# Sliding-window attention in two layers: value products in eight tiles of 64 by 32, queued ahead of the next turn's scores

## The chip, the core and the metric

The kernel runs on one core of a Trainium2 chip. The metric is the time of one execution in device microseconds (us). Engines are named as in the profile: PE is TensorE's matmul stream and PEld its weight loads, DVE is VectorE, ACT is ScalarE, POOL is GpSimd, SP is SyncE, which issues the DMAs here.

## What is computed

Two identical layers over 2048 rows of 640 numbers, each an attention over the last 256 positions with 32 heads of 20 and then a feed-forward part with a squared ReLU:

```python
def _A_ref(x, wqkv, wo):
    H = 32; Dh = D // H; W = 256
    q, k, v = qkv[0], qkv[1], qkv[2]          # of x @ wqkv
    scores = jnp.einsum("bhqd,bhkd->bhqk", q, k) * (Dh ** -0.5)
    mask = (idx[:, None] - idx[None, :] >= 0) & (idx[:, None] - idx[None, :] < W)
    scores = jnp.where(mask[None, None], scores, -1e9)
    p = _softmax(scores, axis=-1)
    o = jnp.einsum("bhqk,bhkd->bhqd", p, v)
    ...
def _B_ref(x, w1, b1, w2, b2):                # relu(x @ w1 + b1) ** 2 @ w2 + b2
    ...
x = x + _A_ref(_layernorm(x, axis=-1), A_wqkv, A_wo)
x = x + _B_ref(_layernorm(x, axis=-1), B_w1, B_b1, B_w2, B_b2)
# and both once more
```

## The kernel before

**Tiling.** A layer's rows are taken in 8 groups of `T` = 256, so there are 16 groups `u`. A query sees the keys of its own group and of the one before (not in the first group of a layer). Dense products (L256) split each operand into a high and a low float16 half and add three products; they are generators that hand out some 500 ns of work at a time. Heads go in quads of four, 8 quads to a group.

**One quad** passes three stages on PE:

- `max_quad` (L511, matmuls L542): scores with queries on the partitions, into two PSUM tiles `bbs[e]` of three banks, one for each half `e` of the array. Four matmuls run side by side on tiles of 64 by 64. Each row of queries has 384 columns of keys, of which the matmuls fill the 320 that a half block of 64 queries can see. DVE adds the mask and takes the row maximum, eight instructions a quad (L555, `tensor_tensor_reduce`), each followed by a read of its accumulator. `max_out` (L561) transposes the maxima and writes them as two more rows of the query operand.
- `exp_quad` (L590, matmuls L613): scores again, now with keys on the partitions, into the same two tiles `bbs[e]`; the maximum is subtracted by the two added rows. ACT takes the exponential out of PSUM in three pieces for each `e` (L625, tile `pt`), and POOL zeroes the triangles outside the window (L640, L644).
- `pv_quad` (L660, matmuls L674): the values in float32 as weights of 32 columns (20 values, a constant that gives the row sum, the rest of the next head), against the exponentials. Four heads run side by side on tiles of 128 by 32. The result `pv` is a PSUM tile of the ring `mm` of two banks, which the dense products use too. ACT copies it out (L686), and for each two quads SP writes it to DRAM (L691), from where `load_o` (L703) loads it for the output projection.

**Order.** The kernel writes out the order of all five engines by hand (`manual_schedule`). `post` (L120) files a job with an engine, a cost in ns and what it depends on; `pump` (L133) emits the jobs that can start, by the kernel's own clock `now`, in order of priority (`prio=0` first). `need` (L150) lets that clock pass until given jobs are done. `banks` (L506) needs all readers of the two score tiles, `bbjobs`. `mm_tile` (L163) needs an empty bank of the ring.

In group 0 `flow` (L971) walks a list of stages and fills in dense work while a stage's inputs are not there. From group 1 on `together` (L935) does it by shares: per turn it emits `exp_quad(n)`, dense work worth 0.55 of a turn, `max_quad(n + 3)`, `pv_quad(n)`, and dense work worth 0.45 of a turn. So PE's queue reads L613, L256, L542, L674, L256, and then the next turn. The dense work is the next group's projections, the output projection of the group before (`stage_o`, L775) and its feed-forward part (`stage_f`, L828). What DVE does for these (residuals L785 and L880, halves L352, L414, L763 and L853, layer norms L273 to L286) stands in its one queue among the maxima.

Of the kernel before, what the change touches and what calls it, by code (L numbers as in the profile page):

```python
# [10 lines left out]
F32 = mybir.dt.float32  # L11
# [5 lines left out]
P = 128  # L17
S = 2048
D = 640
# [11 lines left out]
NQ = H // 4  # L31

# [12 lines left out]
def kernel(ctx: ExitStack, tc: tile.TileContext, x, wqkv, wo, w1, b1, w2, b2, out):  # L45
# [12 lines left out]
    maskb = sb.tile([P, 3 * P], BF16, name="maskb")  # L58
    nc.vector.memset(maskb, 0.0)

    nc.gpsimd.affine_select(out=maskb, in_=maskb, pattern=[[1, 3 * P]], compare_op=ALU.is_gt,
                            fill=NEG, base=0, channel_multiplier=-1)
    nc.gpsimd.affine_select(out=maskb, in_=maskb, pattern=[[-1, 3 * P]], compare_op=ALU.is_ge,
                            fill=NEG, base=2 * P, channel_multiplier=1)
# [427 lines left out]
    def by_turns(ways):  # L492

        t = [0, 0]
        ways = [list(w) for w in ways]
        while ways[0] or ways[1]:
            h = min((h for h in range(2) if ways[h]), key=lambda h: t[h])
            part = ways[h].pop(0)
            t[h] += part[0]
            yield h, part  # L500
# [3 lines left out]
    bbs = [ps.tile([P, 3, 512], F32, name="bb", tag="bb", bufs=2) for e in range(2)]  # L504

# [5 lines left out]
    def max_quad(n):  # L511
# [9 lines left out]
        bb = banks()  # L521

        for w in (3, 0, 1, 2):
            j, i = divmod(w, 2)
            p = 2 * qd + j
            parts = [(prev, 0, T, 0), (cur, 0, P, T)] if i == 0 else [(prev, P, T, 0), (cur, 0, T, P)]
            if g == 0:
                parts = parts[1:]
            if w == 3:
                parts = [(kt, z, z + P, c + z - a) for kt, a, b, c in parts for z in range(a, b, P)]  # L530
            ways = [[], []]
            for kt, a, b, c in parts:
                for h in range(2):
                    lo, hi = (0, 3 * P) if u < 2 else (64 * h, 64 * h + 320)
                    x, y = max(a, a + lo - c), min(b, a + hi - c)
                    if x < y:
                        ways[h].append((y - x, kt, x, y, c + x - a))
            for h, (_, kt, a, b, c) in by_turns(ways):
                for e in range(2):
                    r, m = slice(64 * e, 64 * e + 3 * DH), slice(64 * h, 64 * h + 64)  # L540
                    to = bb[e][m, c // P, 3 * P + c % P:3 * P + c % P + b - a] if w == 3 else bb[e][m, w, c:c + b - a]
# [538 lines left out]
```

## Time and profile before

| | |
|---|---|
| median of 3 runs | 1647.96 us |
| lowest | 1645.14 us |
| the profiled execution's own time | 1641.93 us |
| its span, first to last instruction | 1640.2 us |
| mean granted TensorE clock | 0.987 |
| busy: PE, DVE, ACT, POOL | 1575.6, 1030.1, 748.4, 636.6 us |

The profile is of one execution. A row of a list in order of time gives the start in us from the span's start, the length, the engine, line and operation, what is written and read, and how many instructions follow each other; in brackets how long the engine was idle before and what ended that. A row of a group by line gives shapes, count, busy time, mean ns of one, and the idle time before it. A row of the chain of waits gives start, length and what ran. Matmuls are pipelined and their ends are modelled, so lengths on PE are best read from one start to the next.

### The profile page before, as it was taken

What the parts mean: (1) busy time and instruction counts of PE and PEld (TensorE: products, weight loads), DVE (VectorE), ACT (ScalarE), POOL (GpSimd) and SP (SyncE); (2) the same over time, 40 slices, a digit from 0 to 9 for tenths busy, and PEclk for the clock granted to TensorE, in tenths of its full rate; (3) what the DMA queues carried; (4) which work ended last, traced back from release to release, by engine and by line L of the source; (5) the groups of instructions that cost most, each with busy time, mean ns of one, the idle gap of its engine ahead of it and who ended that gap; (6) DMA issues with size and microseconds to landing.
All of it is one profiled execution on the core that took longest, in us unless ns stands there. A gap on an engine that the chain in (4) does not pass through costs nothing.

```text
span 1640.2 us, 52819 instructions
## 1 busy us (share of the span) xinstructions
PE 1575.6 (96%) x21670; PEld 1172.6 (71%) x21670; DVE 1030.1 (63%) x3231; ACT 748.4 (46%) x1616; POOL 636.6 (39%) x1309
## 2 busy tenths in 40 slices
PE   7697899999999999999999999999999999999989
PEld 5564677777777777777777777777777777776667
DVE  7567657675665766566565756657665666757341
ACT  4465534535444454544434354444545444453512
POOL 1343533535344353434414343443534344354412
PEclk9898999999999999999999999999999999999999
DMA  8465214343342434345253434425343452431020
GB/s 255 123 183 157 62 63 109 65 118 86 102 102 65 124 75 112 80 108 114 51 137 74 124 85 103 102 69 119 73 112 81 106 117 51 110 71 54 27 65 17
DMA packets 231517, 157.95 MB, mean 96 GB/s; under 512 B 79468, under 2 KB 215020, under 8 KB 231276
## 3 DMA queue, kind: packets, MB, share of 16 engines
q1 hardware_dynamic: 231276, 154.59, 38.4%
q8 instruction: 170, 2.79, 0.7%
q14 instruction: 71, 0.58, 0.1%
HBM read 84.68 MB, written 52.95 MB: 84 GB/s over the span
## 4 chain that ended last, share of the span: by engine, by line
PE 83%; DVE 6%; ACT 4%; DMA 4%; POOL 2%; issue 1%; SPq 1%; DVEq 0%; ACTq 0%; POOLq 0%
PE acc L256 63%; PE pv L674 10%; PE bb L542 5%; PE bb L613 5%; DVE bb L555 3%; ACT pt L625 2%; DMA qk<-qd 1%; DMA xt<-in_B_b_dram 1%; PE tr L567 1%; POOL x L805 1%; DVE mx L555 1%; POOL pt L644 0%; ACT r L843 0%; DMA w_s<-in_B_w_dram 0%; DMA ov<-o 0%
## 5 line engine op out<-in xcount | busy, mean ns | idle before, releaser
L555 DVE CUSTOM_DVE_ANT_0 bb<-bb,maskb 128x384 f32<-128x384 f32 (+2 forms) x1024 | 510.5, 567 | 114.9 <-PE bb L542 106.4
L625 ACT ACTIVATE pt<-bb 128x512 f32<-128x512 f32 (+1 forms) x736 | 376.5, 601 | 233.9 <-PE bb L613 220.5
L640 POOL TENSOR_SCALAR_AFFINE_SELECT pt<-pt 128x256 f32<-128x256 f32 x448 | 194.8, 439 | 529.7 <-ACT pt L625 507.9
L256 PE MATMUL acc<-y,w_s 128*128 128x256 f16 x2880 | 330.8, 273 | 4.8 <-DVE y L304 1.5
L256 PE MATMUL acc<-w_s,hh 128*128 128x320 f16 x2304 | 326.2, 299 | 0.0
L256 PEld LDWEIGHTS <-w_s 128*128 128x128 f16 x2880 | 277.9, 98 | 57.3 <-issue 23.5
L256 PE MATMUL acc<-yT,wq_s 128*128 128x256 f16 x2400 | 281.0, 275 | 14.0 <-DVE qd L414 11.9
L256 PEld LDWEIGHTS <-hh 128*128 128x128 f16 x2304 | 221.7, 98 | 96.8 <-issue 12.5
L256 PEld LDWEIGHTS <-wq_s 128*128 128x128 f16 x2400 | 232.9, 99 | 57.5 <-issue 26.5
L644 POOL TENSOR_SCALAR_AFFINE_SELECT pt<-pt 128x256 f32<-128x256 f32 x512 | 217.3, 446 | 65.7 <-ACT pt L625 64.6
L853 DVE TENSOR_TENSOR hh<-r,hh 128x256 f16<-128x256 f32 x192 | 91.9, 500 | 205.9 <-ACT hh L850 199.3
L674 PE MATMUL pv<-pt,vt 128*32 128x128 f32 (+1 forms) x3840 | 189.6, 332 | 2.0 <-POOL pt L644 1.4
L847 POOL TENSOR_TENSOR r<-r 128x256 f32<-128x256 f32 x192 | 113.5, 612 | 181.2 <-ACT r L843 179.9
L686 ACT COPY ot<-pv 128x256 f32<-128x256 f32 x128 | 47.6, 372 | 277.4 <-PE pv L674 277.4
L555 DVE DVE_READ_ACCUMULATOR2_ANT mx<- 128x1 f32 x1024 | 145.4, 142 | 0.1
L256 PE MATMUL acc<-wq_s,yT 128*128 128x320 f16 x960 | 142.1, 301 | 0.1
L674 PEld LDWEIGHTS pv<-pt,vt 128*32 128x32 f32 x3840 | 104.4, 110 | 45.6 <-POOL pt L644 4.9
L256 PE MATMUL acc<-wo_s,od 128*128 128x320 f16 x900 | 130.5, 299 | 3.9 <-DVE x L785 1.7
L843 ACT ACTIVATE r<-acc,b1s 128x256 f32<-128x256 f32 x192 | 80.6, 471 | 98.0 <-PE acc L256 97.2
L256 PEld LDWEIGHTS <-yT 128*128 128x128 f16 x960 | 93.1, 99 | 40.4 <-issue 6.5
L256 PEld LDWEIGHTS <-od 128*128 128x128 f16 x900 | 85.5, 98 | 44.7 <-issue 8.3
L613 PE MATMUL bb<-qt,kt 62*64 62x128 f16 (+3 forms) x3840 | 100.3, 235 | 9.1 <-DVE mx L555 8.4
(84 smaller groups left out, 1169.5 us busy)
## 6 DMA issues: line engine op xcount, KB each, us to landing
qt<-qk SPq DMA_DIRECT2D x30, 480.0 KB
kt<-qk SPq DMA_DIRECT2D x30, 480.0 KB
qk<-qd SPq DMA_DIRECT2D x17, 640.0 KB
o<-ot SPq DMA_DIRECT2D x256, 42.0 KB
od<-o SPq DMA_DIRECT2D x13, 640.0 KB
qk<-yl SPq DMA_DIRECT2D x13, 640.0 KB
qk<-qd SPq DMA_DIRECT2D x17, 320.0 KB
xt<-in_A_x_dram SPq DMA_DIRECT2D x16, 320.0 KB
```

The costliest lines, as they stand in the source:

```text
L256: nc.tensor.matmul(acc, lhs(a, c), rhs(b, c), start=(k == 0), stop=(k == 3 * nk - 1))
L542: nc.tensor.matmul(to, qt[r, p, i * P + 64 * h:i * P + 64 * h + 64], kt[r, p, a:b], start=True, stop=True, tile_position=(64 * e, 64 * h))
L555: nc.vector.tensor_tensor_reduce(out=v, in0=v, in1=mask, scale=1.0, scalar=-3.0e38, op0=ALU.add, op1=ALU.max, accum_out=accum)))
L613: nc.tensor.matmul(bb[e][64 * h:64 * h + 64, k, o:o + w], kt[r, p, ko + 64 * h:ko + 64 * h + 64], qt[r, p, q:q + w], start=True, stop=True ...
L625: nc.scalar.activation(box["pt"][:, :o], bb[e][:, k, :o], AF.Exp, scale=SCALE / (QS * QS))
L640: nc.gpsimd.affine_select(out=m, in_=m, pattern=[[0, 2], [-1, P]], compare_op=ALU.is_gt, fill=0.0, base=0, channel_multiplier=1)
L644: nc.gpsimd.affine_select(out=m, in_=m, pattern=[[0, 2], [1, P]], compare_op=ALU.is_ge, fill=0.0, base=0, channel_multiplier=-1)
L674: nc.tensor.matmul(pv[32 * jj:32 * (jj + 1), q0 * P:(q0 + qn) * P], vf[:, c:c + 32], pj[:, j, :], start=(k == 0), stop=(k == len(steps) - ...
L686: nc.scalar.copy(ot[:, qd % 2], pv)
L843: nc.scalar.activation(box["r"], acc[:, f, :], AF.Relu, bias=b1s[:, f0 + f:f0 + f + 1], scale=1.0 / (YS * WS))
L847: nc.gpsimd.tensor_tensor(box["r"], box["r"], box["r"], op=ALU.mult)
L853: nc.vector.tensor_sub(hh[:, 1, f, :], box["r"], hh[:, 0, f, :])
```

## The change

- **Blocks of 64.** All scores and products go by blocks of 64 keys and 64 queries (`B`). A query block sees five key blocks (`W5` = 320 columns).
- **Packed scores and maxima.** The scores lie packed in the tiles, seen as one row of 1536 columns (`flat`): 4 times 320 for the maxima, 20 blocks of 64 for the exponentials (the table `SPOTS`: for each key block, the first query block, how many, and the place of each of two heads). Columns 1280 to 1535 are left for the values (`pvs`). The mask `maskb` is 320 wide. DVE's eight maxima a quad are over 320 columns (L565). The two tiles are filled with zeros at the start.
- **Exponentials.** ACT takes 1024 and then 256 columns for each `e` (L631). POOL zeroes the triangles in eight instructions a quad, each on 64 partitions (L643). There are two tiles `pt` of 1280 columns in place of six of 512.
- **Values in eight tiles.** A tile is 64 keys by 32 columns: even key blocks in one half of the array, odd ones in the other, each half with its own result (`pvs[0]` in the first score tile, `pvs[1]` in the second). Blocks that the mask empties are left out. `evict_pv` takes the result out: ACT copies the first (L692), DVE adds the second to it (L695), and the writes to DRAM are as before. It is called from the `exp_quad` that follows, after the first two exponentials are filed.
- **Place of the values.** In `together`, `pv_quad(n)` is emitted just ahead of `exp_quad(n + 1)`, after the dense work worth 0.45 of a turn, and it needs `banks()` first. `flow` has the same order.

PE's queue around the values of one quad, in group 4 or so. Before, the last scores for the maxima, then the values (four instructions to a row) and dense work:

```order
L542 LDWEIGHTS qt
L542 MATMUL bb<-kt_79,qt 64x64
L674 MATMUL pv<-pt,vt_89 32x256 x4
L674 MATMUL pv<-pt,vt_86 32x128 x4
L674 MATMUL pv<-pt,vt_95 32x128 x4
L674 MATMUL pv<-pt,vt_92 32x256 x4
L256 LDWEIGHTS wq_s
L256 MATMUL acc<-yT,wq_s 128x256
```

Now, the end of the values and the start of the next scores for the exponentials (the dense work stands ahead of the values):

```order
L673 MATMUL bb<-pt,vt_95 32x192
L673 MATMUL bb<-pt,vt_98 32x192
L673 MATMUL bb<-pt,vt_92 32x64
L673 MATMUL bb<-pt,vt_101 32x64
L622 LDWEIGHTS kt_84
L622 MATMUL bb<-qt,kt_84 64x64
L622 LDWEIGHTS kt_85
L622 MATMUL bb<-qt,kt_85 64x192
```

The values moved from the end of L542 past the dense work to the next turn's scores, from 16 instructions to 32, and they write `bb`. The first of them waits for the seventh maximum of the turn, the second for the eighth.

DVE's queue at the start of the maxima, in the turn in which the projection of the next keys begins (turn F of the prediction; the rows on `mx` alone read the accumulator). Before:

```order
L352 TENSOR_TENSOR yl<-xt,yl 128x640
L286 TENSOR_SCALAR xt<-x_10599,bmv 128x640
L555 ISA bb,mx<-bb,maskb 128x384
L555 ISA mx 128x1
L352 TENSOR_TENSOR yl<-xt,yl 128x640
```

Now:

```order
L565 ISA bb,mx<-bb,maskb 128x320
L565 ISA mx 128x1
L290 TENSOR_SCALAR xt<-x_13073,bmv 128x640
L418 SCALAR_TENSOR_TENSOR yl<-acc,yl 128x2x256
L565 ISA bb,mx<-bb,maskb 128x320
L565 ISA mx 128x1
L356 TENSOR_TENSOR yl<-xt,yl 128x640
```

The normalisation (L286, now L290) moved from ahead of the maxima to behind the first of them, and a cast of keys (L418) stands there too; a second one stands behind the fifth maximum, where before it stood behind the eighth. In the other turns of a group, in the order A to H, there now stand among the maxima: nothing; one residual L889; nothing; two casts L418; one residual L794; (F); nothing; nothing.

The core of the diff:

```diff
+B = 64
+W5 = 5 * B
...
+    flat = [b.rearrange("p k n -> p (k n)") for b in bbs]
+    pvs = [b[:, 2, T:] for b in bbs]
+    for b in bbs:
+        nc.vector.memset(b, 0.0)
...
-        for w in (3, 0, 1, 2):
+        ways = [[], []]
+        for w in range(4):
             j, i = divmod(w, 2)
...
+        for h, (n, kt, k, p, q, o) in by_turns(ways):
+            for e in range(2):
+                r = slice(B * e, B * e + 3 * DH)
+                keys = cur[r, p, 0:1].to_broadcast([3 * DH, n]) if kt is None else kt[r, p, k:k + n]
+                nc.tensor.matmul(flat[e][B * h:B * h + B, o:o + n], qt[r, p, q:q + B], keys,
+                                 start=True, stop=True, tile_position=(B * e, B * h))
...
+                v, mask = flat[e][:, W5 * w + o:W5 * (w + 1)], maskb[:, o:]
+                bbjobs.append(post("D", 113 + 1.047 * (W5 - o), lambda v=v, mask=mask, accum=accum:
...
+    SPOTS = {(b, j): (q, n, at[j]) for b, q, n, *at in (
+        (0, 0, 1, 0, 5), (4, 0, 4, 1, 16), (6, 2, 2, 6, 11), (2, 0, 3, 8, 13),
+        (5, 1, 3, 0, 5), (1, 0, 2, 3, 8), (7, 3, 1, 10, 15), (3, 0, 4, 11, 16)) for j in range(2)}
...
+        for o, w in ((0, 1024), (1024, 256)):
             for e in range(2):
...
+                    if o == 0:
+                        tiles[e] = sb.tile([P, 20 * B], F32, name="pt", bufs=2)
+                    nc.scalar.activation(tiles[e][:, o:o + w], flat[e][:, o:o + w], AF.Exp, scale=SCALE / (QS * QS))
+
+                last[e] = post("A", 50 + 0.834 * w, power, last.get(e))
+                bbjobs.append(last[e])
+            if o == 0:
+                evict_pv()
...
     def pv_quad(n, quad):
         u, qd = divmod(n, NQ)
-        steps = steps_of(u)
-        pv, jobs = mm_tile([P, T], "pv")
...
+        banks()
+        tiles, masks = quad
+        need(*masks)
+        ways, first = [[] for _ in range(8)], [None] * 8
...
+        for z, (w, b, at, q) in by_turns(ways):
+            jj, h = divmod(z, 2)
...
+            nc.tensor.matmul(pvs[h][32 * jj:32 * (jj + 1), q * B:q * B + w], vf[B * h:B * h + B, c:c + 32],
+                             tiles[e][B * h:B * h + B, at * B:at * B + w],
+                             start=left[z] == len(ways[z]) - 1, stop=left[z] == 0, skip_group_check=True,
+                             tile_position=(B * h, 32 * jj))
+        now[0] += 1250.0 if u % NG else 800.0
+        leaving.append(n)
+
+    def evict_pv():
+        if not leaving:
+            return
...
+        def low():
+            nc.scalar.copy(ot[:, qd % 2], pvs[0])
+
+        def high():
+            nc.vector.tensor_tensor(ot[:, qd % 2, q0:], pvs[1][:, q0:], ot[:, qd % 2, q0:], op=ALU.add)
...
+        bbjobs.append(post("D", 350, high, post("A", 262, low), prio=0))
...
         for k, (part_, what, m) in enumerate(ts):
-            if what and what[0] == "s":
-                quad = exp_quad(what[1])
+            if what:
+                if held_v:
+                    pv_quad(*held_v.pop())
+                held_v.append((what[1], exp_quad(what[1])))
...
-            if what and what[0] == "v":
-                pv_quad(what[1], quad)
```

More of the change, by code (lines that the diff above doesn't have):

```diff
@@ L57 @@
     nc.vector.memset(neghalf, -0.5)
-    maskb = sb.tile([P, 3 * P], BF16, name="maskb")
+    maskb = sb.tile([P, W5], BF16, name="maskb")
     nc.vector.memset(maskb, 0.0)
[L61 to L64, printed above, removed]
+    for h in range(2):
+        half = maskb[64 * h:64 * h + 64]
+        nc.gpsimd.affine_select(out=half, in_=half, pattern=[[1, W5]], compare_op=ALU.is_gt,
+                                fill=NEG, base=0, channel_multiplier=-1)
+        nc.gpsimd.affine_select(out=half, in_=half, pattern=[[-1, W5]], compare_op=ALU.is_ge,
+                                fill=NEG, base=T, channel_multiplier=1)
     b1s = sb.tile([P, FC], F32, name="b1s")
@@ new lines, in exp_quad, with mask @@
+                last[e] = post("A", 50 + 0.834 * w, power, last.get(e))
+                bbjobs.append(last[e])
+            if o == 0:
+                evict_pv()
+        for h, own, at in ((0, 1, 1), (1, 1, 0), (0, 0, 0), (1, 0, 4)):
+            if not own and u % NG == 0:
+                continue
+            for e in range(2):
+                def mask(e=e, h=h, own=own, at=at):
+                    m = tiles[e].rearrange("p (a n) -> p a n", n=B)[B * h:B * h + B, at::5, :]
+                    nc.gpsimd.affine_select(out=m, in_=m, pattern=[[0, 4], [1 if own else -1, B]],
+                                            compare_op=ALU.is_ge if own else ALU.is_gt, fill=0.0, base=0,
+                                            channel_multiplier=-1 if own else 1)
+                masks.append(post("G", 375, mask, last[e]))
@@ L660, in pv_quad @@
+        return tiles, masks
     def pv_quad(n, quad):
         u, qd = divmod(n, NQ)
[L662 to L678 removed]
+        banks()
@@ new lines, in pv_quad @@
+        tiles, masks = quad
+        need(*masks)
+        ways, first = [[] for _ in range(8)], [None] * 8
+        for (b, j), (q, nb, at) in blocks_of(u).items():
+            for e in range(2):
+                z = 2 * (2 * j + e) + b % 2
+                part = (nb * B, b, at, q)
+                if b in (4, 3 if u % NG else 5):
+                    first[z] = part
+                else:
+                    ways[z].append(part)
+        for z in range(8):
+            ways[z] = [first[z]] + sorted(ways[z], key=lambda p: p[0] * (1 if z // 2 % 2 else -1))
@@ L961, in together @@
                 done += c
-            if what is None:
+            if what is None and k >= 2 * len(ns):
                 for it in late:
```

156 lines of the change are left out of this document (51 added, 105 removed).

## The prediction, made before the changed kernel was run

> **What bounds the kernel now.** I read the page first, then the chain of waits, then the lists of TensorE and VectorE in order of time over one group of 256 rows in the steady middle (497 to 592 us), and last the groups by line and shape.
>
> ```profile
> PE 1575.6 (96%) x21670; PEld 1172.6 (71%) x21670; DVE 1030.1 (63%) x3231; ACT 748.4 (46%) x1616; POOL 636.6 (39%) x1309
> PE 83%; DVE 6%; ACT 4%; DMA 4%; POOL 2%; issue 1%; SPq 1%; DVEq 0%; ACTq 0%; POOLq 0%
> ```
>
> TensorE is busy 96% of the span and is 83% of the chain that ends last. In the middle of the program it is nearly all of it, and the chain there is TensorE's own queue, piece after piece (start, length, what):
>
> ```profile
> 504.74 0.68 PE bb L613 x25
> 505.42 5.00 PE acc L256 x36
> 510.42 0.68 PE bb L542 x20
> 511.10 1.44 PE pv L674 x32
> 512.54 3.91 PE acc L256 x28
> 516.45 0.68 PE bb L613 x25
> ```
>
> So one turn is: scores for the exponentials (L613) 0.68, dense products 5.00, scores for the maxima (L542) 0.68, values (L674) 1.44, dense 3.91, next turn's scores. What adds to TensorE's queue, as work or as a wait, adds to the time. The question for the change is what else has little room. VectorE reduces the maxima (L555) out of the same PSUM tiles into which the next turn's L613 writes. Here each row is one turn, from the start of L542 to the start of the next L613; the columns are the stretch, its length, and VectorE's busy time on L555 alone:
>
> ```profile
> 498.09:504.67 6.58, 4.22 (x16) 1.00 0.30 85
> 510.35:516.38 6.03, 4.23 (x16) 1.00 0.27 54
> 522.16:528.19 6.03, 4.23 (x16) 1.00 0.26 60
> 534.44:540.49 6.05, 4.33 (x16) 1.00 0.36 114
> 546.40:552.71 6.31, 4.31 (x16) 1.00 0.90 180
> 558.26:564.88 6.62, 4.26 (x15) 1.00 0.63 102
> 570.78:577.40 6.62, 4.23 (x16) 1.00 0.66 193
> 583.10:589.15 6.05, 4.22 (x16) 1.00 0.02 4
> ```
>
> I call these turns A to H. The maxima need 4.2 us of a stretch of 6.0 to 6.6, and they can't begin before the scores are done. VectorE's own rows: turn B, the first of D, then F with what stands before and between its maxima:
>
> ```profile
> 511.26 0.57 DVE L555 CUSTOM_DVE_ANT_0 bb<-bb,maskb 128x384 f32<-128x384 f32 x1
> ...
> 515.35 0.15 DVE L555 DVE_READ_ACCUMULATOR2_ANT mx<- 128x1 f32 x1
> 515.40 0.49 DVE L880 SCALAR_TENSOR_TENSOR x<-acc,x 128x320 f32<-128x320 f32 x1
> 515.81 1.55 DVE L352 TENSOR_TENSOR yl<-xt,yl 128x640 f16<-128x640 f32 x2
> ...
> 535.25 0.57 DVE L555 CUSTOM_DVE_ANT_0 bb<-bb,maskb 128x384 f32<-128x384 f32 x1 [1.10 <-PE bb L542]
> ...
> 558.53 0.61 DVE L286 TENSOR_SCALAR xt<-x,bmv 128x640 f32<-128x640 f32 x1 [0.44 <-POOL bmv L284]
> 559.07 0.57 DVE L555 CUSTOM_DVE_ANT_0 bb<-bb,maskb 128x384 f32<-128x384 f32 x1
> ...
> 561.77 0.69 DVE L414 SCALAR_TENSOR_TENSOR yl<-acc,yl 128x512 f16<-128x512 f32 x1
> 562.38 0.56 DVE L555 CUSTOM_DVE_ANT_0 bb<-bb,maskb 128x384 f32<-128x384 f32 x1
> ...
> 564.91 0.14 DVE L555 DVE_READ_ACCUMULATOR2_ANT mx<- 128x1 f32 x1
> ```
>
> The first maximum starts 0.81 us (D) to 0.91 us (B) after L542, eight follow at (515.35 - 511.26) / 8 = 0.51, and the last is out 5.15 us after L542 in B, where the next L613 comes at 6.03. In F three other instructions stand among the maxima, the last one is out at 6.79, and L613, which came at 6.62, did wait. All such waits together are small now (us in total, times, the longest):
>
> ```profile
> PE bb L613 <- DVE mx L555: 8.4, 11, 3.0
> ```
>
> **The change, part by part.** *Values in eight tiles.* Now four column tiles run side by side, each through all 128 keys: (256 + 128 + 128 + 256) columns in two passes.
>
> ```profile
> L674 PE MATMUL pv<-pt,vt 128*32 128x256 f32 x1920 | 155.2, 390 | 0.3
> ```
>
> 768 columns take 1.44 us, or 1.67 ns a column (1.28 us) plus 0.16 for the start and the change of tile shape. Per tile the change leaves 10 of 12 half blocks, 640 columns: 1.07 + 0.16, and 0.02 to 0.03 because eight tiles start one after another instead of four: 1.25 us. The gain is 0.19 us in each of the 112 turns that look back (in the 16 of a layer's first group the longest tile stays at 384 columns): **-21 us**. The trace shows no 64x32 tiles. If the two halves of the array took turns, a turn would cost 2 x 1.07 + 0.16 = 2.3 us, +96 us in all; the best is -24 us. I take -21, since L542 runs on tiles of both halves (36 matmuls in the 0.68 us above) with no such loss.
>
> The Trainium skill, page "TensorE: Matmul & The Clock Gate", section "Wait — 56ns, not 53.3ns?", says that matmuls never start closer than about 25 ns apart. By it the 64 pieces that a turn now has would need 1.6 us and the change would cost about 36 us here instead of saving 21. The row of L542 speaks against it (at most 0.68 us / 36 = 19 ns apart on tiles side by side).
>
> *Scores.* The columns per tile stay at 1280 in both kinds, except in group 1, where 384 become 320: 8 turns x 2 x 4 x 64 columns at 0.42 ns, **-2 us**. There are 38 pieces for the maxima instead of 36: nothing, within 0.03 us a turn.
>
> *Maxima.* Eight of 320 columns for eight of 384.
>
> ```profile
> L555 DVE CUSTOM_DVE_ANT_0 bb<-bb,maskb 128x384 f32<-128x384 f32 x896 | 469.3, 591 | 97.5 <-PE bb L542 94.0 <-issue 3.0
> L555 DVE CUSTOM_DVE_ANT_0 bb<-bb,maskb 128x128 f32<-128x128 f32 x64 | 18.1, 323 | 17.4 <-PE bb L542 12.4 <-ACT w_s L194 3.2 <-ACT pt L625 1.1
> ```
>
> (591 - 323) / 256 = 1.05 ns a column, so 0.51 becomes 0.447 and eight take 3.58 us.
>
> *The values wait for the maxima.* Their result now lies in the third bank of the two score tiles, and they are queued ahead of the next turn's L613, behind the same dense stretch. So they, no longer L613, must wait for the last maximum of the turn, and they come 1.44 us earlier in it. Dense products and that L613 are queued behind; nothing on TensorE can pass. Ready time after L542: 0.9 for the first maximum + 3.58 + 0.2 (the last read, 0.15, and the hand-over) = 4.7 us, plus what VectorE's queue now has among the eight: in B and E one residual (L880's kind, 515.81 - 515.40 = 0.41), in D two query casts (0.61, as 562.38 - 561.77 in F, and about half of it for the one of 256 columns), in F the normalisation (559.07 - 558.53 = 0.54), two casts (0.61 each) and one low half (0.78, half of the pair in B). TensorE arrives at the stretch less 1.44. Waits: A (5.14) 0.55, B (4.59) 0.5, C (4.59) 0.1, D (4.61) 1.05, E (4.87) 0.25, F (5.18) 2.05, G (5.18) 0, H (4.61) 0.1. A stands apart: four casts of the feed-forward part run first and end late.
>
> ```profile
> 498.26 2.07 DVE L853 TENSOR_TENSOR hh<-r,hh 128x256 f16<-128x256 f32 x4 [4.69 <-ACT hh L850]
> ```
>
> They end at 500.3, so the first maximum is 2.2 after L542 (498.09); the change keeps these four there, and I take 1.9. The sum is 4.6 us a group. The first groups and the last two have shorter dense stretches and would wait longer, but hold the waits of L613 above and others that this one replaces; group 0 I leave at nothing for its waits on loads. 15 x 4.6 = **+69 us**. Bounds: 0 if VectorE is always through in time, and 7 us a group (+105) if the inserted casts also wait for ScalarE.
>
> *Exponentials and masks.* Six of 512 columns become two of 1024 and two of 256.
>
> ```profile
> 505.47 3.04 ACT L625 ACTIVATE pt<-bb 128x512 f32<-128x512 f32 x6 [0.69 <-PE bb L613]
> 512.63 0.37 ACT L686 COPY ot<-pv 128x256 f32<-128x256 f32 x1 [0.67 <-PE pv L674]
> ```
>
> 2560 / 3072 of 3.04 is 2.5 us, plus the values' copy 0.37, and a new add on VectorE of about the same. Together with the 0.69 from L613 to the first exponential that is under 4 us of the 5.7 that lie between L613 and L542 (504.67 to 510.35), covered by the dense 5.00; were that gone, it would be 0.37 a turn. The masks, as many as before and on half the partitions, have until the values, a dense stretch later than now: nothing. The buffers of the exponentials go from six to two, and the next turn's must wait until the values have read these; the values stand ahead of its scores in TensorE's own queue: nothing. L542 now also waits for the values' copy and add, since they read its tile; they are inside the 4 us.
>
> *Clearing the score tiles at the start.*
>
> ```profile
> 1.68 2.11 DVE L83 MEMSET kt<- 128x512 f32 x4
> ```
>
> Two fills of 1536 columns come behind these four of 512 in VectorE's queue, ahead of the statistics of the first rows, with which all work begins; nothing covers them: 2.11 x 3072 / 2048 = **+3 us**.
>
> The sum is -21 - 2 + 69 + 3 = +49 us on the profiled execution's 1641.9 us (its span is 1640.2): 1691. The median of the runs is 1648.0, 6 us above that execution, so I forecast **1697 us**.
>
> **The rivals.** *The wait does not bite.* If VectorE is through before TensorE arrives, only -20 is left: 1642 - 20 + 6 = 1628, not slower. Its place is the start of the values, its price the 69 us, and it decides from 20 / 15 = 1.3 us a group downwards. For it: C, G and H have no or little excess by my sum, ScalarE has half a microsecond more in each turn, and a long wait in one turn lets VectorE clear its queue for the next. Against it: D and F alone give 3.1, and the same sum for the present F (0.81 + 4.1 + 0.2, and 0.61 + 0.78 of insertions) gives 6.5, where the trace has 6.79: the sum errs short. Chance 0.27, from 1628 to 1672.
>
> *Eight tiles do not run side by side.* The values then cost up to 2.3 us a turn: 1691 + 21 + 96 + 6 = 1814. L542's 0.68 us speaks against it. Chance 0.07, and of this 0.02 for a floor at the start of matmuls, at about 1755.
>
> *The attention output comes late.* Four writes for every two quads go to SP's queue behind the copy and the add. The eighth quad's values now leave after the next group's first scores, some 7 us later (a dense stretch of 3.91, a copy behind two exponentials), and the loads for the output projection wait for these writes.
>
> ```profile
> L753 DVE RECIPROCAL rs<-rs 128x64 f32<-128x64 f32 x64 | 33.9, 537 | 1.5 <-DMA rs<-o 1.5
> ```
>
> Today that wait is 1.5 us in all, so there is room; 3 us a group would give 1697 + 42 = 1739. Chance 0.08.
>
> **How the numbers follow.** Forecast 0.58 with its own range from 1672 (3 us a group) to 1727 (6.6 us a group). For 8 in 10 I reach to 1650 and 1745, which leaves out the lower part of the first rival and most of the second. A measurement here tells about 2% (33 us) from no change. Slower by more: 0.48 of the forecast's 0.58, and the last two rivals, 0.15, together 0.63. Within: 0.34. Faster by more needs more than the whole gain of the values: 0.03.
>
> **What would show it.** In the profile after: a turn's values at 1.2 to 1.3 us (2.3: second rival); TensorE idle before the values, put down to the maxima's line, 50 to 100 us in all, with F the longest at about 2 us and G at none (under 20 us: first rival); no wait of L613 on maxima; L542 without waits on the copies of the values; eight turns at about 100 us (now seven take 85.0, from 498.09 to 583.10, so eight take 97).

## The result, and the profile after

The changed kernel takes 1773.3 us in the median (1769.2 to 1775.5), the kernel before on the same chip 1646.6: the ratio is **1.077 [1.074, 1.080]**. One of the four runs of the kernel before took 3175.8 us, and the ratio leaves it out. The forecast was 1697 us with a range from 1650 to 1745. So the direction was right, and the loss is 2.6 times the 49 us of the sum.

The profiled execution has a span of 1767.4 us against 1640.2, 127.2 more. From its page and from its list of waits (us in total, times, the longest):

```profile
PE 1616.9 (91%) x25862; PEld 1228.4 (70%) x25862; DVE 1015.4 (57%) x3361; ACT 704.3 (40%) x1392; POOL 647.5 (37%) x1311
```

```profile
PE bb L673 <- DVE mx L565: 81.3, 59, 11.8
```

TensorE's share has fallen from 96% to 91%: it now waits, and the largest entry is the one that the prediction named, values (L673) on maxima (L565). One of the 59 waits, of 11.8 us, is at the start of the program, where ScalarE, and behind it VectorE, wait for the DMA `qk<-qd`; before the change the dense products (L256) waited 11.9 us for the same, by way of L414. So some 70 us are new. VectorE has less work than before (1015 us, 1030 before) and yet sets the pace here.

TensorE's own list over turns A, B, F, G and the next A of the same middle stretch, only the values and the scores behind them:

```profile
539.92 1.92 PE L673 MATMUL bb<-pt,vt 64*32 64x256 f32 x64 [0.27 <-DVE mx L565]
541.77 0.75 PE L622 MATMUL bb<-qt,kt 62*64 62x64 f16 x32
...
552.17 1.92 PE L673 MATMUL bb<-pt,vt 64*32 64x256 f32 x64
554.02 0.75 PE L622 MATMUL bb<-qt,kt 62*64 62x64 f16 x32
...
605.54 1.92 PE L673 MATMUL bb<-pt,vt 64*32 64x256 f32 x64 [2.67 <-DVE mx L565]
607.39 0.75 PE L622 MATMUL bb<-qt,kt 62*64 62x64 f16 x32
618.39 1.52 PE L673 MATMUL bb<-pt,vt 64*32 64x256 f32 x64
619.84 0.75 PE L622 MATMUL bb<-qt,kt 62*64 62x64 f16 x32
...
643.20 1.92 PE L673 MATMUL bb<-pt,vt 64*32 64x256 f32 x64 [0.27 <-DVE mx L565]
```

Three things are to be read here. Eight turns take 643.20 - 539.92 = 103.3 us (97 before, about 100 forecast). A turn that waits for nothing, G, takes 619.84 - 618.39 = 1.45 us for its values, as long as before (1.44), not 1.25. And a turn that waits takes 1.85 (A: 541.77 - 539.92), also where no wait is printed ahead of it (B): there is a second wait, of 0.40, inside the values. The two halves of the array write into two score tiles, each half waits for the last maximum of its own tile, and these two come one maximum apart (0.45 us, 605.26 to 605.71 in the next list). The first instruction of the values starts behind the one, the second behind the other, and all the rest stand behind the second in the queue.

VectorE in turn F, and GpSimd in the same turn:

```profile
598.45 0.50 DVE L565 CUSTOM_DVE_ANT_0 bb<-bb,maskb 128x320 f32<-128x320 f32 x1 [0.37 <-PE bb L555]
598.86 0.14 DVE L565 DVE_READ_ACCUMULATOR2_ANT mx<- 128x1 f32 x1
600.22 0.61 DVE L290 TENSOR_SCALAR xt<-x,bmv 128x640 f32<-128x640 f32 x1 [1.21 <-POOL bmv L288]
600.75 0.68 DVE L418 SCALAR_TENSOR_TENSOR yl<-acc,yl 128x512 f16<-128x512 f32 x1
601.35 0.49 DVE L565 CUSTOM_DVE_ANT_0 bb<-bb,maskb 128x320 f32<-128x320 f32 x1
...
605.26 0.14 DVE L565 DVE_READ_ACCUMULATOR2_ANT mx<- 128x1 f32 x1
605.26 0.53 DVE L565 CUSTOM_DVE_ANT_0 bb<-bb,maskb 128x320 f32<-128x320 f32 x1
605.71 0.14 DVE L565 DVE_READ_ACCUMULATOR2_ANT mx<- 128x1 f32 x1
```

```profile
595.58 0.41 POOL L643 TENSOR_SCALAR_AFFINE_SELECT pt<-pt 64x256 f32<-64x256 f32 x1 [2.65 <-ACT pt L631]
596.16 3.39 POOL L643 TENSOR_SCALAR_AFFINE_SELECT pt<-pt 64x256 f32<-64x256 f32 x7 [0.17 <-ACT pt L631]
599.63 0.55 POOL L288 TENSOR_TENSOR bmv<-bmv,neghalf 128x1 f32<-128x1 f32 x1
```

Between its first and its second maximum VectorE stands still for 1.21 us: the next instruction in its queue is a normalisation that needs a power from GpSimd (L288), and this stands behind the turn's eight masks, which end at 599.55. Before the change the same stop was 0.44 us (in the row of L286 that the prediction shows).

Where the 127 us lie is seen by comparing when each turn's exponential scores start in the two traces (no view gives this in one row; it is worked out from the starts of L613 and L622, turn by turn):

| stretch of the program | more than before, us |
|---|---|
| to the first scores | 4.0 |
| groups 0 and 1 | 14.8 + 1.7 |
| groups 2 to 6 | 30.7 (6.1 each) |
| groups 7 and 8 | 4.8 + 6.4 |
| groups 9 to 13 | 28.2 + 6.1 (6.9 each) |
| group 14, and 7 turns of the last | 9.4 + 14.6 |
| after the last turn's scores | 6.5 |

The mean granted TensorE clock is also lower, 0.978 against 0.987. As an estimate from these and the two spans, some 39 us of full clock are missing against 21 before, so at most some 18 of the 127 us come with the lower clock. No run separates that from the waits.

### The profile page after: what moved, and what is told of

Same layout as the page of the kernel before. It is cut to its first block, busy times and chain, and to the rows that moved or that the text cites. A ratio compares the mean times of both kernels' runs of the same rounds, so it can differ in the third digit from the quotient of the medians.

```text
span 1767.4 us, 60949 instructions
## 1 busy us (share of the span) xinstructions
PE 1616.9 (91%) x25862; PEld 1228.4 (70%) x25862; DVE 1015.4 (57%) x3361; ACT 704.3 (40%) x1392; POOL 647.5 (37%) x1311
## 5 line engine op out<-in xcount | busy, mean ns | idle before, releaser
L643 POOL TENSOR_SCALAR_AFFINE_SELECT pt<-pt 64x256 f32<-64x256 f32 x960 | 408.0, 442 | 727.0 <-ACT pt L631 705.5
L631 ACT ACTIVATE pt<-bb 128x1024 f32<-128x1024 f32 (+1 forms) x512 | 346.6, 711 | 446.9 <-PE bb L622 353.8
L565 DVE CUSTOM_DVE_ANT_0 bb<-bb,maskb 128x320 f32<-128x320 f32 (+2 forms) x1024 | 452.5, 505 | 112.7 <-PE bb L555 112.1
L673 PE MATMUL bb<-pt,vt 64*32 64x256 f32 (+3 forms) x7680 | 227.0, 311 | 89.6 <-DVE mx L565 81.3
L673 PEld LDWEIGHTS bb<-pt,vt 64*32 64x32 f32 x7680 | 155.6, 108 | 160.3 <-issue 119.2
L862 DVE TENSOR_TENSOR hh<-r,hh 128x256 f16<-128x256 f32 x192 | 95.5, 520 | 134.3 <-ACT hh L859 128.5
L695 DVE TENSOR_TENSOR ot<-bb,ot 128x256 f32<-128x256 f32 (+1 forms) x128 | 52.2, 408 | 202.4 <-ACT ot L692 200.8
L565 DVE DVE_READ_ACCUMULATOR2_ANT mx<- 128x1 f32 x1024 | 143.1, 140 | 0.0
L555 PE MATMUL bb<-kt,qt 60*64 60x64 f16 (+3 forms) x4704 | 97.3, 222 | 4.8 <-ACT pt L631 4.5
L555 PEld LDWEIGHTS <-qt 60*64 60x64 f16 x4704 | 74.6, 108 | 37.0 <-issue 36.4
```

Of the source, the lines that this page charges most:

```text
L555: nc.tensor.matmul(flat[e][B * h:B * h + B, o:o + n], qt[r, p, q:q + B], keys, start=True, stop=True, tile_position=(B * e, B * h))
L565: nc.vector.tensor_tensor_reduce(out=v, in0=v, in1=mask, scale=1.0, scalar=-3.0e38, op0=ALU.add, op1=ALU.max, accum_out=accum)))
L631: nc.scalar.activation(tiles[e][:, o:o + w], flat[e][:, o:o + w], AF.Exp, scale=SCALE / (QS * QS))
L643: nc.gpsimd.affine_select(out=m, in_=m, pattern=[[0, 4], [1 if own else -1, B]], compare_op=ALU.is_ge if own else ALU.is_gt, fill=0.0, base=0,
L673: nc.tensor.matmul(pvs[h][32 * jj:32 * (jj + 1), q * B:q * B + w], vf[B * h:B * h + B, c:c + 32], tiles[e][B * h:B * h + B, at * B:at * B ...
L695: nc.vector.tensor_tensor(ot[:, qd % 2, q0:], pvs[1][:, q0:], ot[:, qd % 2, q0:], op=ALU.add)
```

## The experiments

All ratios are to the kernel before, measured on the same chip. Line numbers are those of each run's own kernel.

### The wait for the maxima

**The last quarter first.** The edit, in scores and maxima:

```diff
-        for w in range(4):
+        for w in (3, 0, 1, 2):
```

> The scores and the maxima of a turn are made in the order last quarter, first, second, third, and nothing else is changed. The values' result shares its PSUM bank with the last quarter alone, so the values now wait for the first two of a turn's eight maxima instead of the last two. Theory (the values wait for the maxima, twice in a turn): the idle time before the values goes (75 us in the trace of the changed kernel, of which 12 are a wait for the first loads that stays), and the second wait inside the values, for the eighth maximum, goes too (the 128 runs of values take 228 us together; without a wait one takes 1.45, and 0.80 in a layer's first group, 175 in all; some 10 of the difference belong to the last turns, which wait for masks). 1773 - 63 - 43 = 1667 us, up to 1690 if in turn F the next scores now wait up to 1.5 us for the same maxima. Rival (the wait only moves from the values to the next scores, since VectorE is behind): no more than 30 us are won, 1743 or above. Rival (the time lies in the eight tiles themselves): 1760 or above, and the values still take 1.85 us in most turns.

Measured 1776.0 us, 1.079 [1.078, 1.081], and the same waits:

```profile
PE bb L673 <- DVE mx L565: 81.5, 58, 12.5
```

Read by the expectation this would be the rival about the tiles. But the rows show that the edit did not take the wait away: the values start behind the seventh and eighth maximum as before, although these now read other banks. What the program waits for is the whole score tile. The run says nothing for or against the theory.

**A tile of its own.**

```diff
-    bbs = [ps.tile([P, 3, 512], F32, name="bb", ...) for e in range(2)]
-    pvs = [b[:, 2, T:] for b in bbs]
+    bbs = [ps.tile([P, 2, 512], F32, name="bb", ...) for e in range(2)]
+    bts = [ps.tile([P, 512], F32, name="bt", ...) for e in range(2)]
+    pvs = [b[:, T:] for b in bts]
...
+            o = B if g and w == 3 else o0
```

> The order of the last-quarter-first run did not take the wait away: the values still waited for the seventh and the eighth maximum, whichever these were, so the dependence is on the whole score tile and not on its third bank. Here that bank is a tile of its own (two tiles of two banks for the first 1024 columns, two of one bank for the last 256 and the values' result). The last quarter's scores and maxima come first, and its maxima leave out the first 64 of its 320 keys, which lie in the other tile; the order on VectorE, ScalarE, GpSimd and SyncE's queue stays as in the changed kernel. The values then wait for no maximum of the other three quarters. Theory (the wait for the maxima is what the change costs): the 63 us of idle time before the values and some 43 inside them go, less up to 20 us for waits of the next scores on the same maxima in turn F and at the ends: 1667 to 1690 us. Rival (the wait hides others: with TensorE earlier by 6 us a group, the output projection waits for the attention output instead, 3 us a group as in the run of the place alone, and the next scores wait in F): 1700 to 1740. Rival (nothing but a shift of the waits): 1750 or above.

Measured **1693.6 us, 1.029 [1.027, 1.031]**: 80 us less than the changed kernel. Two turns of it, and its largest wait of TensorE on VectorE:

```profile
595.12 1.52 PE L679 MATMUL bt<-pt,vt 64*32 64x256 f32 x64
596.57 0.64 PE L628 MATMUL bb<-qt,kt 62*64 62x64 f16 x28
...
606.89 1.52 PE L679 MATMUL bt<-pt,vt 64*32 64x256 f32 x64
608.33 0.64 PE L628 MATMUL bb<-qt,kt 62*64 62x64 f16 x28
```

```profile
PE bb L628 <- DVE mx L571: 29.9, 34, 11.3
```

In the middle groups the values now take 1.45 us and none waits. The theory is right within 4 us of its upper end. What is left of the wait has gone to the next scores (L628): 29.9 us, 11.3 of them the wait at the start of the program, and in F 1.0 us a group ahead of them, since the maxima of F come late for these too. So the wait for the maxima, outside and inside the values, is worth 80 us, net of what moves on.

### The order of the values' pieces

**Waves of equal width**, alone (first run) and with the last quarter first (second):

```diff
-            ways[z] = [first[z]] + sorted(ways[z], key=lambda p: p[0] * (1 if z // 2 % 2 else -1))
+            ways[z] = [first[z]] + sorted(ways[z], key=lambda p: -p[0])
```

> The changed kernel with only the order of the values' pieces changed, to waves of equal width; the wait for the last two maxima stays. Theory (the two halves of the array wait for the seventh and the eighth maximum, 0.45 us apart, and the second half then needs its 640 columns): a turn that waits still takes 0.43 us more than one that does not, and all turns save what the order costs, 0.2 us: 1773 - 22 = 1751 us. Rival (the order costs nothing): 1768 or above.

> The last quarter first, and besides the pieces of the values in an order in which all eight tiles take a piece of the same width at a time (256, 192, 128, 64 columns). Theory (with mixed widths the instruction at the head of TensorE's queue waits for a tile that is still busy, and pieces for free tiles stand behind it): a turn's values take 1.25 us instead of 1.45, 112 x 0.2 = 22 us less than with the last quarter first alone, about 1645 to 1668. Rival (64 pieces in a turn cost what they cost, whatever their order): the same as with the last quarter first alone within 5 us, and 1.45 us a turn.

Measured 1761.6 us, 1.072 [1.070, 1.074], and 1763.8 us, 1.072 [1.070, 1.074]. From the first run's list, one turn that does not wait:

```profile
615.11 1.37 PE L673 MATMUL bb<-pt,vt 64*32 64x256 f32 x64
616.41 0.75 PE L622 MATMUL bb<-qt,kt 62*64 62x64 f16 x32
```

The values take 616.41 - 615.11 = 1.30 us instead of 1.45, for the same 64 matmuls: the order costs 0.15 us a turn. That is less than the 0.2 of the theories, and the first run lies between its theory and its rival. Of 112 x 0.15 = 16 us the times show 12 in both pairs (1773.3 to 1761.6, 1776.0 to 1763.8); the waits stay, in the second run too, since the last quarter first does not remove them.

**Own tile and equal waves together.**

> The same with the values' pieces in waves of equal width. In the two runs with such waves a turn without a wait took 1.30 us instead of 1.446, so the theory gives 112 x 0.145 = 16 us less than the run with its own tile, if nothing else then waits: 1651 to 1674 us. If TensorE is ahead of the other engines without that, less than 6 us are won.

Measured 1686.8 us, 1.025 [1.022, 1.027]: 7 us of the 16. The values take 1.30 us throughout, but TensorE then meets other waits sooner, the next scores in F among them (1.0 becomes 1.2 us).

### The place

**The place alone**, in the kernel before, with the values' four tiles and their own bank:

```diff
-            if what and what[0] == "v":
-                pv_quad(what[1], quad)
...
+            if what:
+                if held_v:
+                    pv_quad(*held_v.pop())
+                held_v.append((what[1], exp_quad(what[1])))
```

> The kernel before, with its values in four tiles of 128 by 32 in a bank of their own, and only their place in the order changed: behind the rest of the dense products and ahead of the next turn's scores, as in the change. Theory (the place alone costs nothing, what costs is that the result lies in the bank that the maxima read): 1640 to 1660 us. Rival (the later place itself delays the output projection, the masks or the copies): 1670 or above.

Measured 1718.9 us, 1.045 [1.042, 1.048]. The rival is right:

```profile
473.94 3.55 PE L256 MATMUL acc<-wo_s,od 128*128 128x320 f16 x13 [3.13 <-DVE od L763]
...
490.61 1.51 PE L674 MATMUL pv<-pt,vt 128*32 128x256 f32 x32 [0.96 <-DVE yl L414]
```

The output projection waits 3.1 us a group for the attention output, and the values wait for a free bank of the ring `mm`, into which they write here and which at this place casts of VectorE hold (11.5 us in all, as in the row) or an activation of ScalarE (10.1 us). These three waits make 58 of the 83 us that the profiled execution has more; the rest was not taken apart. The later place is not free in the old kernel. The second cost is not in the change, which left that ring. The first is not in its middle groups either; from the changed kernel's list of waits:

```profile
PE acc L260 <- ACT od L769: 10.4, 5, 4.1
PE acc L260 <- DVE od L772: 0.6, 2, 0.3
```

These waits stand in group 8, the first of the second layer, and from group 14 on.

**The old place**, with own tile and equal waves: values, copy and add directly behind the turn's scores for the maxima.

```diff
-            yield 1 - SHARE, None, m
+            yield 1 - SHARE, ("v", n), m
...
+            if what and what[0] == "v":
+                pv_quad(*held_v.pop())
+                evict_pv()
```

> The kernel with its own tile and equal waves, but the values at their place of before, directly behind the turn's scores for the maxima, with their copy and add right behind. There they must wait for the first two maxima of that turn: 0.9 us to the first, 2 x 0.38, and 0.2, less the 0.7 that the scores take: 1.16 us in 112 turns, 130 us, of which up to 25 come back because the next scores and the output projection no longer wait. Theory: 1687 + 130 - 25 = 1792, up to 1817 us. Rival (the later place is itself what costs, and VectorE's maxima are early enough): 1690 or below.

Measured 1912.6 us, 1.163 [1.162, 1.165], 95 us above the theory. Two turns, and its two largest waits:

```profile
659.23 1.72 PE L679 MATMUL bt<-pt,vt 64*32 64x256 f32 x64 [0.38 <-DVE mx L571]
...
673.33 0.59 PE L679 MATMUL bt<-pt,vt 64*32 64x256 f32 x2 [1.65 <-DVE mx L571]
675.24 2.74 PE L679 MATMUL bt<-pt,vt 64*32 64x256 f32 x62 [1.32 <-POOL pt L649]
```

```profile
PE bt L679 <- DVE mx L571: 104.3, 114, 3.2
PE bt L679 <- POOL pt L649: 43.5, 40, 3.6
```

The wait for two maxima is there, and it is the larger one. The theory had left out the second wait, for masks (L649), which at this place are not done. The mean granted clock is lower too, 0.954 against 0.979 in the run with the same tile and waves; as an estimate from the two spans that is up to 52 us, and how much of the excess it is was not measured. So the packed kernel needs the later place for its maxima and for its masks.

### Turn F, GpSimd and the masks

**The power first**, in the changed kernel and in the one with own tile and equal waves:

```diff
-                                                                   op=ALU.pow), j, prio=prio)
+                                                                   op=ALU.pow), j, prio=0)
```

> The changed kernel with one priority changed: the power that a normalisation needs from GpSimd (L288) goes ahead of the masks that the planner has not yet queued. In turn F of the changed kernel it stands behind all eight masks of the turn (595.58 to 599.55 us), which can only begin when the last short exponentials are out, and VectorE, whose queue holds the normalisation ahead of the second maximum, stands still for 1.21 us for it. Theory (F's wait comes from GpSimd's queue, by way of VectorE's): the power stands behind three masks of F instead of eight, the 1.21 us go in 13 groups, 1773 - 16 = 1757 us, and the values of F wait 1.5 us instead of 2.74. Rival (VectorE's own work makes the maxima late): 1768 us or above, F as before.

> The same priority in the kernel with its own tile and equal waves (1687 us). There the wait of F stands at the next scores, 1.17 us in 13 groups, and VectorE stands still 1.60 us for the power. Theory: 13 x 1.17 = 15 us less, 1672 us, no wait of the next scores in F. Rival (the rest of VectorE's work fills the gap): 1682 or above.

Measured 1770.3 us, 1.077 [1.075, 1.079], and 1678.4 us, 1.021 [1.019, 1.023]. In the first run F still waits:

```profile
608.46 1.92 PE L673 MATMUL bb<-pt,vt 64*32 64x256 f32 x64 [2.36 <-DVE mx L565]
```

2.36 instead of 2.67. The power stood behind six masks of F, not three as I had expected, and VectorE still stopped for 1.20 us, now ahead of its first maximum. The first run gained 3 us of 16, as its rival has it; the second gained 8 of 15.

**Exponentials by tile.** The first edit has the copy of the values (`evict_pv`) behind all four exponentials, the second between the two tiles.

```diff
-        for o, w in ((0, 1024), (1024, 256)):
-            for e in range(2):
-                def power(e=e, o=o, w=w):
+        for e in range(2):
+            def power(e=e):
+                for o, w in ((0, 1024), (1024, 256)):
...
-        for h, own, at in ((0, 1, 1), (1, 1, 0), (0, 0, 0), (1, 0, 4)):
+        for e in range(2):
+            for h, own, at in ((0, 1, 1), (1, 1, 0), (0, 0, 0), (1, 0, 4)):
```

> The changed kernel with the exponentials of one score tile after those of the other (1024 and 256 columns of the first, then of the second), the copy of the values behind all four, and the masks of the first tile ahead of those of the second. In the changed kernel the masks need the two short exponentials, which stand behind both long ones and the copy, so the first mask of F starts 3.5 us after the turn's scores (2.0 before the change). Here the first tile's masks can start about 1.5 us earlier. Theory (F's wait comes from the late masks, which hold up the power on GpSimd and with it VectorE): the power comes up to 1.5 us earlier, VectorE's stop of 1.21 us in F goes, F's wait falls from 2.74 to about 1.5 us, 13 x 1.2 = 16 us, and the last three turns, which wait for masks, gain some 3 us: 1773 - 19 = 1754 us. Rival (as the priority of the power alone, which gained 3 us: VectorE is full in F whatever GpSimd does): 1766 or above.

> Own tile, equal waves, the power first (1678 us together) and the exponentials by tile. Theory: the next scores' remaining wait in F (0.79 us in 13 groups) goes, and up to 1.5 us in each of the last three turns: 1678 - 13 = 1665 us, still above the kernel before. Rival (nothing left to win there): 1675 or above.

> The exponentials by tile again, but with the copy of the values between the two tiles' exponentials instead of behind all four. In the run with the copy behind all four (1822 us), TensorE waited 2.8 us a group for the attention output, which the changed kernel does not, so that run changed two things at once. Here the copy comes earlier than in the changed kernel (behind 1280 columns of exponentials instead of 2048) and the first tile's masks come earlier too. Theory (late masks hold up the power, VectorE and the values of F): no wait for the attention output in the middle groups, F's wait 1.5 us instead of 2.74, 1773 - 16 = 1757 us or below. Rival (the masks' time does not matter, VectorE is full): F as before, 1768 to 1775 us. Second rival (grouping the exponentials itself delays the output by the order it gives VectorE): 1800 or above, with the 2.8 us still there.

> Own tile, equal waves and the power first (1678 us together), with the exponentials by tile and the copy between. Theory: no wait for the attention output in the middle groups, the next scores' wait in F (0.79 us) goes: 1678 - 10 = 1668 us or below. Second rival as above: 1695 or above.

Measured, copy behind: 1822.4 us, 1.109 [1.106, 1.112], and 1700.4 us, 1.034 [1.032, 1.036]. Both theories fell. The copy of F starts 3.3 us after the turn's scores instead of 2.75, and TensorE waits for the attention output, as in the run of the place alone (first run):

```profile
PE acc L260 <- DVE od L771: 32.1, 14, 2.8
```

Copy between: 1788.4 us, 1.085 [1.082, 1.089], and 1671.6 us, 1.016 [1.014, 1.018]. There is no such wait now in the middle groups, so the copy, which came half a microsecond later, made it, and the second run comes within 4 us of its theory. But the first is still slower than the changed kernel, and F waits 2.3 us: the first masks are earlier, but the eighth still ends 6.7 us after the turn's scores began (7.5 in the changed kernel), the power behind it, and VectorE stops for 1.41 us. None of these runs took the stop away, so none tests it.

**Without the power, and without the masks**, both in the changed kernel, and **the kernel before without masks** as the control.

```diff
-        j = post("G", 520, lambda: nc.gpsimd.tensor_tensor(box["mv"][:, 3:4], ... op=ALU.pow), j, prio=prio)
-        j = post("D", 576, lambda: nc.vector.tensor_scalar(y, src, box["mv"][:, 0:1], box["mv"][:, 3:4],
+        j = post("D", 576, lambda: nc.vector.tensor_scalar(y, src, box["mv"][:, 0:1], box["mv"][:, 2:3],
```

```diff
+        masks += last.values()
-        for h, own, at in ((0, 1, 1), (1, 1, 0), (0, 0, 0), (1, 0, 4)):
+        for h, own, at in ():
```

```diff
-                    ms.append(post("G", 375, mask, ex))
+                    ms.append(ex)
```

> The changed kernel without the power on GpSimd: the normalisation multiplies by the scaled variance itself, so this part of the computation is changed and VectorE no longer waits there for GpSimd. In the two runs that made the power or the masks earlier, VectorE still stood for 1.2 to 1.4 us in F, only ahead of the first maximum instead of behind it, so they did not test that stop. Theory (of F's 3.17 us, 2.74 before the values and 0.43 inside, 1.2 come from the stop, the rest from VectorE's own instructions as forecast): F's wait before the values is 1.4 to 1.7 us, 13 groups save 1.0 to 1.3 each, 1756 to 1760 us. Rival (VectorE is full without the stop): F 2.3 us or more, 1766 or above.

> The changed kernel without the eight masks of a turn, which are left out of the computation; GpSimd is then free for the power at once, and the values wait for no mask. Theory (GpSimd's queue is what holds up the power): the same as without the power, and the last three turns, which wait 1.6, 2.9 and 3.2 us inside their values for masks, save these: 1748 to 1753 us. Rival (the stop in F is the power's own run, 0.55 us, and its two hand-overs, not its place behind the masks): F 2.3 us or more, and only the 8 us at the end are saved, 1765 us.

> The kernel before without its masks, which are left out of the computation as in the run before this one: the control for it. That run was 48 us below the changed kernel. Theory (the change makes masks that cost nothing cost something, since they end later and stand in front of the power and of the values): here at most 10 us are saved, 1635 to 1647 us, so that some 38 us or more of the 48 belong to the change. Rival (masks cost that much in both kernels): 1610 or below.

Measured without the power 1756.5 us, 1.068 [1.066, 1.070]; without masks **1725.5 us, 1.049 [1.048, 1.051]**; before without masks 1637.5 us, 0.995 [0.993, 0.997]. F without the power:

```profile
602.38 1.92 PE L671 MATMUL bb<-pt,vt 64*32 64x256 f32 x64 [1.87 <-DVE mx L563]
```

and without masks, VectorE's stop and TensorE's wait (the row has the first 31 of the 64 matmuls):

```profile
593.14 0.62 DVE L290 TENSOR_SCALAR xt<-x,bmv 128x640 f32<-128x640 f32 x1 [0.44 <-POOL bmv L288]
```

```profile
598.96 1.30 PE L674 MATMUL bb<-pt,vt 64*32 64x256 f32 x31 [1.33 <-DVE mx L565]
```

Without masks the stop is 0.44 us, as before the change, and F's wait falls by 1.34 us, from 2.67 to 1.33; without the power it falls by 0.80, more than the priority gave and less than expected, although the time of that run lies in the theory's range. In both runs the planner's order of VectorE in F changes as well: the normalisation now stands ahead of the first maximum. Without masks that order is the one of the run with the power first, where F waits 2.36, so 1.0 us of the 1.34 belong to the masks and the rest to the order and the power's place. So the masks ahead of the power make some two fifths of F's wait. Over the whole program the masks cost 48 us in the changed kernel and 8 in the kernel before: some 40 us of the change are theirs (with what their absence changes in the order), by F, by the last three turns, and by smaller waits. They are not to be added to the 80, since part of them is the same waiting.

### Maxima alone

The kernel before with `max_quad` and `maskb` of the change, the rest as it was:

```diff
-                bbjobs.append(post("D", 113 + 1.047 * (3 * P - o), ...
+                v, mask = flat[e][:, W5 * w + o:W5 * (w + 1)], maskb[:, o:]
+                bbjobs.append(post("D", 113 + 1.047 * (W5 - o), ...
```

> The kernel before with one part of the change alone: the scores for the maxima packed to five blocks of 64 keys and maxima of 320 columns instead of 384; exponentials, masks and values stay as they were, values in their old place and bank. Theory (VectorE does not set the end before the change; only the 8.4 us of waits of the next scores on maxima can go): 1637 to 1647 us. Rival (the packed scores, 38 pieces instead of 36 and other keys, cost TensorE more): 1650 or above. Rival (a faster VectorE frees banks earlier all over): 1630 or below.

Measured **1636.1 us, 0.995 [0.993, 0.996]**, 0.5% below the kernel before and just below the theory's range:

```profile
PE 1570.3 (96%) x22022; PEld 1173.2 (72%) x22022; DVE 974.4 (60%) x3231; ACT 749.7 (46%) x1616; POOL 632.4 (39%) x1311
```

```profile
PE bb L620 <- DVE mx L562: 4.5, 4, 2.7
```

VectorE has 56 us less to do and the time falls by 7. Of the 8.4 us of waits of the next scores on maxima that stood in the profile before, 4.5 are left, so these waits give about 4 of the 7. By the starts of the scores, as in the table above, groups 3 to 13 take as long as before, and the gain lies at the two ends. So in the middle of the kernel before, the width of the maxima costs nothing.

## Why the prediction was wrong

**Values, -21 us: the term was mis-sized.** The eight tiles do run side by side (the second rival is out), but with the pieces in the order of the change they take 1.45 us, so nothing is gained; in equal waves 1.30, where I had 1.25. The step that failed is "640 columns: 1.07 + 0.16". It counted columns per tile as if no tile ever stood idle. Pieces of 192, 128 and 64 columns follow each other in one queue, and a piece for a free tile stands behind one for a busy tile. The Trainium skill, page "TensorE: Matmul & The Clock Gate", section "The mechanism", has matmuls start in strict order of the program; the 0.15 us between the two orders agree with it. The floor of about 25 ns between starts that the prediction cites from the Trainium skill would make, as an estimate, 1.6 us of 64 matmuls; 1.45 and 1.30 us, 23 and 20 ns each, do not agree with it.

**The wait for the maxima, +69 us: right mechanism, too small.** The run with a tile of its own shows 80 us, net. By turn, wait ahead of the values and (second number) time above 1.45 inside them, against the forecast: A 0.27 + 0.40 (0.55), B 0 + 0.40 (0.5), C 0 + 0.11 (0.1), D 0.89 + 0.39 (1.05), E 0 + 0.23 (0.25), F 2.67 + 0.40 (2.05), G and H none (0, 0.1): 5.8 us where the sum had 4.6. The rows of C, D and E are not shown; their numbers come from the same list. All of the excess is in A, D and F, and 1.0 of it in F. The prediction's upper bound, 7 us a group "if the inserted casts also wait for ScalarE", looked for the right thing at the wrong engine: it was GpSimd.

**Masks, "nothing": failed.** I counted how many there are and that the values need them late. I did not ask what else stands in GpSimd's queue. The two short exponentials come behind the long ones and the copy, the first mask of F starts 3.5 us after its scores (592.09 to 595.58), the power waits for all eight, VectorE waits for the power, and seven maxima wait behind it.

**The ends, "group 0 I leave at nothing": failed.** The prediction took the longer waits of the first and the last groups to be paid by waits that they replace. Groups 0 and 1 lose 16.5 us, group 14 and the last seven turns 24, the end 6.5. In the last three turns the values wait for masks inside:

```profile
PE bb L673 <- POOL pt L643: 6.7, 3, 2.9
```

These waits are gone in the run without masks. For group 0 no run was made. The run with its own tile still loses 10 of the 16.5 in groups 0 and 1, so most of it is not the wait for the maxima. Group 0 by itself loses 10.7 to 20.5 us in every run with the values in eight tiles, 17.9 in the one without masks; the maxima alone (-1.6) and the place alone (0.8, with the order of group 0 left as it was) do not lose it. What it is stays open.

**What held.** A maximum takes 0.45 us, as forecast. No scores wait for maxima, and L555 has hardly a wait for the copies. The fills cost 3 us:

```profile
14.96 1.44 PE L260 MATMUL acc<-yT,wq_s 128*128 128x256 f16 x6 [0.84 <-DVE yT L308]
```

```profile
12.10 2.29 PE L256 MATMUL acc<-yT,wq_s 128*128 128x256 f16 x10 [0.84 <-DVE yT L304]
```

(the same products after and before). The first rival, that the wait does not bite, is out. The third, a late attention output, is not what happens in the middle groups of the change, but its price was right: about 3 us a group, in the run of the place alone and in the two with the copy behind all exponentials.

Groups 2 to 13 lose 76 us, 6.4 a group, where the sum's 3.1 a group gave 37. Of the difference, 1.5 a group are the values' gain that did not come and 1.2 the longer waits; the remaining 0.6 was not traced. The two ends lose 51 us, where the sum gave 12. With one repair on another, the times go from 1773.3 to 1693.6 (own tile), 1686.8 (equal waves), 1678.4 (the power first) and 1671.6 us (exponentials by tile, the copy between). This best version with the values in eight tiles is still 27 us above the kernel before: by the same comparison of its turns 9 up to the end of group 1, 10 in groups 2 to 13, and 9 behind them. Those 27 were not taken apart.

## What to carry to other kernels

Before moving work next to a resource, ask what unit the program waits for: here two results that never overlap waited for each other because they shared a tile, and a tile of its own gave back 80 of 127 us. Price a packed group of small matmuls by its waves, with the widest piece of each, not by the columns per tile. And when an engine's work is as much as before but starts later, read what stands behind it in that engine's queue, on GpSimd too: masks that cost 8 us became masks that cost 48.

## What the runs showed of the hardware beside that

- 64 matmuls on eight tiles of 64 by 32 (32 float32 instructions, two matmuls in the profile for each), take 1.30 us from their first start to the next instruction's in waves of equal width, and 1.45 us with the widths mixed.
- An instruction that waits at the head of TensorE's queue holds up all behind it, for other tiles too: in F of the changed kernel the first instruction of the values starts at 605.54 us on one maximum, the second at 605.99 on the next, and the other 30 follow the second.
